# Retention and two feed-forward layers: the next pair's scores ahead of the outer products, and the work of the weights around them in another order

## Chip, cores and metric

One Trainium2 chip, one NeuronCore. The metric is device time in microseconds of the whole program; the runs shown of the kernel before have a median of 1027.86 us (1026.41, 1027.86 and 1028.14). The profile is one further execution.

## What is computed

```
def _attn_ref(q, k, v):                      # 4 batches, 8 heads, 768 positions, 64 wide
    for t in range(S):
        state = gamma * state + outer(k[:, :, t], v[:, :, t])
        y[:, :, t] = scale * q[:, :, t] @ state
def _moe_ref(x, w_in, w_out):                # 3072 tokens, 512 -> 2048 -> 512
    h = x @ w_in
    return np.maximum(0.01 * h, h) @ w_out
def _moe2_ref(x, w_in, w_out):               # the same shapes
    h = x @ w_in
    return (h * (1.0 / (1.0 + np.exp(-1.702 * h)))) @ w_out
reference = _moe2_ref(_moe_ref(tokens of _attn_ref, ...), ...)
```

The weights arrive as 64-bit floats, so each 512 KB piece of the first layer's weights has to be turned into single precision on the chip before it is used.

## The kernel before

**Retention.** The 768 positions of a batch are cut into 6 chunks of 128; 4 batches make 24 steps. Step s loads one block of 1 MB (`a_load`, L276): q and k with the head dimension on the partitions, then k and v by rows, 256 KB each. Five blocks lie in a ring (`in_ring`, the tile h in the rows). The parts of a step are:

- `a_scores` (L282): 16 matmuls into PSUM (L290) and the product with the decay mask on VectorE (L293) into one of two buffers
- `a_decay` (L296): 8 scalings of k on ScalarE (L301), not in a batch's last chunk
- `a_sum` (L313): 16 matmuls (L319) that add the chunk's k-v products to the state in PSUM; `a_state` (L330): the state scaled on VectorE (L333)
- `a_inner` (L322): 16 matmuls (L327) of the masked scores with v; `a_outer` (L336): 16 matmuls (L341) of q with the state, not in a batch's first chunk
- `a_store` (L346): the product with the decay of q on VectorE (L356, six instructions a pair, or L369, two a pair). Steps 0 to 3 are the first layer's input `x0`, which ScalarE (L365) and GpSimd (L157) also split into a high and a low part.

The main loop (L411) takes two steps, s and t = s + 1, a pair p = s / 2. In it, beside retention, 16 pieces of the first layer's weights (n = 0 to 15) are made ready: `load_raw` (L171) loads one into a ring of three; `work_scalar` (L210) makes two ScalarE passes (L178, L179) over it into a ring of three (`a_ring`); `work_vector` (L219) three VectorE passes (L182, L184, L186); `work_last` (L227) the rounding (L195, on GpSimd for the first two pieces, on VectorE after), four GpSimd subtractions for every second piece (L157) into `made`, and `finish` of the piece before (L197: a ScalarE cast L160 and a VectorE subtraction L157, high and low part of a matmul's weight). `factors_out` (L205) writes `made`, 512 KB, to DRAM from GpSimd's queue. `ffn_in` (L245) then multiplies a finished piece with `x0`: 12 matmuls (L253) into bank 7 or 0, a ScalarE pass (L257) and a DMA of 256 KB from ScalarE's queue.

Every engine executes its instructions in the order of the program text; nothing is reordered. In a pair that order is: scores of s and t; one piece's `work_scalar`, `work_vector`, `work_last`; the next piece's `work_scalar`; up to two `ffn_in`; sum and inner of s, its state; the next piece's `work_vector`; inner and sum of t; outer of s; state of t; outer of t; decays of the next pair; store of s; the next piece's `work_last`; store of t; loads of two later steps.

```
        loads = {0: (4, 5), 2: (6, 7), 4: (8, 9), 6: (10, 11, 12)}.get(s, (s + 5, s + 6))
```

The sixteen `ffn_in` stand in pairs 3 to 11 (`now_in`, L203). Behind the loop, the same weights are multiplied with `x1` (L1010), and two layers follow that take most of the time and that the diff does not touch.

Of the kernel before, what the change touches and what calls it, by code (L numbers as in the profile page):

```python
# [25 lines left out]
NC = S // P  # L26
KF = DFF // P
TB = 512
CPB = TB // P
N_STEPS = B * NC  # L30
# [27 lines left out]
QT = 2 * P  # L58
# [32 lines left out]
def retention_two_ffn(ctx: ExitStack, tc: tile.TileContext, qkv, consts, small, w1i, w1o, w2i, w2o, scratch, out):  # L91
    nc = tc.nc
# [63 lines left out]
    def subtract(o, x, y, e=nc.vector):  # L156
        e.tensor_tensor(out=o, in0=x, in1=y, op=ALU.subtract)  # L157

    def split(hi, lo, src, eng=nc.vector):
        nc.scalar.copy(out=hi, in_=src)  # L160
        subtract(lo, src, hi.bitcast(F32), eng)
# [9 lines left out]
    def load_raw(m):  # L171
        raw[m] = t = next(raw_ring).bitcast(U32)
        nc.sync.dma_start(out=t, in_=w1i[m].bitcast(U32).rearrange("p (f two) -> p f two", two=2))
# [20 lines left out]
    def round_up(f, low, e=nc.vector):  # L194
        e.tensor_tensor(out=f.bitcast(I32), in0=f.bitcast(I32), in1=low.bitcast(I32), op=ALU.add)  # L195
# [3 lines left out]
        wt[m] = t = home["h1"].view(8 * (m % NQ) + 4 * (m // NQ), 2, 512)  # L199
        split(t[:, 0], t[:, 1], a)  # L200

    P0 = 2
    now_in = {p: [m for m in (2 * p - 7, 2 * p - 6) if 0 <= m < KF] for p in range(N_STEPS // 2)}  # L203

    def factors_out(q):  # L205
        nc.gpsimd.dma_start(out=wdt[q], in_=made)

    made = e4.view(0, 4, QT)

    def work_scalar(n):  # L210
        if n + 2 < KF:
            load_raw(ORDER1[n + 2])
        if n < KF:
            t = raw.pop(ORDER1[n])
            a = next(a_ring).bitcast(U32)
            words_scalar(a, t[:, :, 0], t[:, :, 1])
            conv[ORDER1[n]] = a, t[:, :, 0], t[:, :, 1]

    def work_vector(n):  # L219
        if n < KF:  # L220
            a, _, high = conv[ORDER1[n]]
            for step in words_vector:
                step(a, high)
        if n and n % 2 == 0 and n <= KF:
            factors_out(n // 2 - 1)

    def work_last(n):  # L227
        if n < KF:
            a, low, _ = conv[ORDER1[n]]
            round_up(a, low, nc.gpsimd if n < 2 else nc.vector)  # L230
            f = a.bitcast(F32)
            if n % 2:
                b11, b21 = work_last.f[:, :QT], work_last.f[:, QT:]
                b12, b22 = f[:, :QT], f[:, QT:]
                for o, x, y in ((made[:, 3], b12, b11), (made[:, 2], b12, b22), (made[:, 1], b22, made[:, 3]),
                                (made[:, 0], b21, made[:, 1])):
                    subtract(o, x, y, nc.gpsimd)
            work_last.f = f
        if 0 < n <= KF:
            finish(ORDER1[n - 1])  # L240

# [3 lines left out]
    def ffn_in(m, x, cols, ring, queue=nc.scalar):  # L245
        n = cols.stop - cols.start
        h = banks[:, h_banks[i_h[0] % len(h_banks)], :n]
        i_h[0] += 1
        w = wt[m].rearrange("p s (k f) -> p s k f", k=NP)
        i = 0  # L250
        for k in range(NP):
            for a, c in ((0, 1), (0, 0), (1, 0)):
                nc.tensor.matmul(out=h, lhsT=w[:, a, k], rhs=x[c][:, k], start=(i == 0), stop=(i == 3 * NP - 1),  # L253
                                 skip_group_check=True)
                i += 1
        t = next(ring)[:, :n]
        nc.scalar.activation(out=t, in_=h, func=AF.Lrelu)  # L257
        queue.dma_start(out=gd1[m][:, cols], in_=t)

    def retention():  # L260
# [12 lines left out]
        ins, sc_t, ks_t = {}, {}, {}  # L273
        kv = banks[:, 2, : NP * D].rearrange("p (n d) -> p n d", n=NP)

        def a_load(s):  # L276
            ins[s] = next(in_ring)
            parts = ((0, 2), (3, 4)) if steps[s][1] == NC - 1 else ((0, 2), (2, 4)) if s < 3 else ((0, 4),)
            for i, j in parts:
                nc.sync.dma_start(out=ins[s][:, i:j], in_=qkv[s, :, i:j])  # L280

        def a_scores(s):  # L282
            t = ins[s]
            qT = t[:, 0].rearrange("p (n i) -> p n i", n=NP)
            kT = t[:, 1].rearrange("p (n i) -> p n i", n=NP)
            ps = (banks[:, 5:7] if s % 2 else banks[:, 0:2]).rearrange("p e (n i) -> p e n i", n=NP)
            for n in range(NP):
                for e in range(2):
                    r = slice(D * e, D * e + D)
                    nc.tensor.matmul(out=ps[:, e, n], lhsT=kT[r, n], rhs=qT[r, n], start=True, stop=True,  # L290
                                     skip_group_check=True)
            sm = next(sm_ring)
            nc.vector.tensor_tensor(out=sm, in0=ps, in1=mask, op=ALU.mult)  # L293
            sc_t[s] = sm
# [51 lines left out]
        def a_store(s, o):  # L346
            b, c = steps[s]
            if c % 3 == 0:
                a_store.x = next(x_ring)
            blk = min(s // CPB, 2) if s < NC else 2  # L350
            cols = slice(s * P, s * P + P)
            x = x1_raw[:, :, s % CPB * P : s % CPB * P + P] if blk == 1 else a_store.x[:, :, c % 3 * P : c % 3 * P + P]

            def put(r, u, t):
                n = 2 * P
                nc.vector.tensor_tensor(out=x[r].rearrange("p (m u) i -> p u m i", u=2)[:, u],  # L356
                                        in0=o[t, u, :n].rearrange("p (m i) -> p m i", i=P),
                                        in1=qdec[t].rearrange("p (m u) i -> p u m i", u=2)[:, u], op=ALU.mult)

            if blk < 2 or b == B - 1:  # L360
                put(slice(0, P), 0, slice(0, P))
                for r, t in halves:
                    put(r, 1, t)
            if blk == 0:
                nc.scalar.copy(out=x0[0][:, :, cols], in_=x)  # L365
                subtract(x0[1][:, :, cols], x, x0[0][:, :, cols].bitcast(F32), nc.gpsimd)
            if blk < 2 or b == B - 1:
                return
            nc.vector.tensor_tensor(out=x.rearrange("p (m u) i -> p u m i", u=2),  # L369
                                    in0=o[:, :, : 2 * P].rearrange("p u (m i) -> p u m i", i=P),  # L370
                                    in1=qdec.rearrange("p (m u) i -> p u m i", u=2), op=ALU.mult)
            if c % 3 == 2:
                a_store.due = xd0[b][c // 3], a_store.x
# [22 lines left out]
            for _ in range(n):  # L396
                nc.tensor.matmul(out=warm, lhsT=idle[:, :P], rhs=idle, start=True, stop=True, skip_group_check=True)

        def a_end(s, o):
            a_store(s, o)  # L400
            if a_store.due:
                nc.sync.dma_start(out=a_store.due[0].rearrange("n p c -> p n c"), in_=a_store.due[1])
                a_store.due = None

        keep_warm(8)
        a_scores(0)
        a_decay(0)
        a_decay(1)
        last = len(steps)
        units = iter(range(KF + 1))  # L410
        for s in range(0, last, 2):  # L411
            t, p = s + 1, s // 2
            mine = [n for n in itertools.islice(units, 2)] if p >= P0 else []
            if s:
                a_scores(s)
                a_scores(t)
            if mine:
                work_scalar(mine[0])
                work_vector(mine[0])
                work_last(mine[0])  # L420
            if len(mine) > 1:
                work_scalar(mine[1])
            i_h[0] = 0
            for m in now_in[p]:
                ffn_in(ORDER1[m], x0, slice(0, TB), g_ring)
            if not s:
                keep_warm(6)
            a_sum(s)
            a_inner(s)
            a_state(s)  # L430
            if not s:
                a_scores(t)
                keep_warm(6)
            if len(mine) > 1:
                work_vector(mine[1])
            a_inner(t)
            a_sum(t)
            o = a_outer(s)
            a_state(t)
            o2 = a_outer(t)  # L440
            for k in (s + 2, s + 3):
                if k < last:
                    a_decay(k)
            a_end(s, o)
            if len(mine) > 1:
                work_last(mine[1])
            a_end(t, o2)
            loads = {0: (4, 5), 2: (6, 7), 4: (8, 9), 6: (10, 11, 12)}.get(s, (s + 5, s + 6))
            for n, k in enumerate(loads):
                if k < last:  # L450
                    a_load(k)
                if n == 0 and s in (0, 2):
                    load_raw(ORDER1[s // 2])
            if p in (3, 4):
                k = slice(2 * p - 6, 2 * p - 4)
                split(x1[0][:, k], x1[1][:, k], x1_raw[:, k])
            for k in (s, t):
                for step in beside_steps.get(k - last, ()):
                    step()
# [864 lines left out]
```

## Time and profile before

| what | value |
|---|---|
| median of the runs shown | 1027.86 us |
| the profiled execution's own time | 1025.9 us |
| its span | 1024.2 us |
| TensorE busy | 1008.8 us, 99% |
| VectorE busy | 812.9 us, 79% |
| ScalarE busy | 607.9 us, 59% |
| GpSimd busy | 175.6 us, 17% |
| mean DMA rate | 232 GB/s |
| end of the retention loop on TensorE | 133.78 us |

The span runs from the first to the last instruction. Busy time counts an instruction from its start to its modelled end. The time that matters for this change lies in the first 134 us, which are read from rows in order of time on each engine: start, length, line, tiles, and in square brackets how long the engine stood idle ahead of the row and what ended that.

### The profile page before, as it was taken

How to read it: one execution, taken by the hardware profiler on the slowest of the kernel's cores; microseconds unless marked ns; L12 is line 12 of the kernel's file. 1: busy time of each engine (PE TensorE's matmuls, PEld its weight loads, DVE VectorE, ACT ScalarE, POOL GpSimd, SP SyncE). 2: the span in 40 equal slices, each digit the busy share in tenths (PEclk: the TensorE clock that was granted, in tenths of full speed). 3: DMA queues.
4: the chain of work that ended last, by engine and by line, in shares of the span. 5: the costliest groups of instructions: out<-in, count | busy, mean ns of one | idle time of the engine just before them, and what ended most of it. 6: DMA issues, size and time to landing. Idle time of an engine off the chain costs nothing.

```text
span 1024.2 us, 17017 instructions
## 1 busy us (share of the span) xinstructions
PE 1008.8 (99%) x5857; PEld 866.3 (85%) x5857; DVE 812.9 (79%) x1396; ACT 607.9 (59%) x1197; POOL 175.6 (17%) x304
## 2 busy tenths in 40 slices
PE   8899999999999999999999999999999999999998
PEld 6687799999999888888888888888888888888886
DVE  4988788987875998998989775554676997988986
ACT  5766556675666665555547765545666555455452
POOL 2432223333333000000000222222232000000000
PEclk9999999999999999999999999999999999999999
DMA  9899959979787846537454984664797646536524
GB/s 352 338 367 390 346 185 314 373 246 327 247 303 284 297 124 223 184 121 262 162 164 171 335 298 161 211 246 147 251 342 271 220 125 146 164 111 143 164 75 83
DMA packets 163814, 237.36 MB, mean 232 GB/s; under 512 B 58768, under 2 KB 103568, under 8 KB 161552
## 3 DMA queue, kind: packets, MB, share of 16 engines
q1 hardware_dynamic: 137408, 161.65, 49.2%
q0 software_dynamic: 19104, 69.62, 17.6%
q10 hardware_dynamic: 7216, 5.02, 1.5%
q8 instruction: 46, 0.75, 0.3%
q14 instruction: 40, 0.33, 0.1%
HBM read 143.95 MB, written 92.27 MB: 231 GB/s over the span
## 4 chain that ended last, share of the span: by engine, by line
PE 89%; DVE 4%; DMA 2%; ACT 2%; POOL 1%; issue 1%; ACTq 0%; DVEq 0%; POOLq 0%
PE psum L837 45%; PE psum L646 38%; PE psum L253 3%; ACT h L301 1%; DMA c<-w1i 1%; POOL e L157 1%; DVE b L293 1%; PE psum L327 1%; DMA wdt<-e 1%; DVE a L356 1%; PE psum L319 0%; PE psum L290 0%; DMA h<-qkv 0%; DVE h L157 0%; PE psum L341 0%
## 5 line engine op out<-in xcount | busy, mean ns | idle before, releaser
L837 PE MATMUL psum<-c,h 128*128 128x512 f32 x1008 | 228.9, 389 | 0.0
L837 PEld LDWEIGHTS psum<-c,h 128*128 128x128 f32 x1008 | 189.1, 188 | 39.2
L837 PE MATMUL psum<-b,h 128*128 128x512 f32 x768 | 179.3, 389 | 0.0
L837 PEld LDWEIGHTS psum<-b,h 128*128 128x128 f32 x768 | 144.2, 188 | 29.9
L659 POOL DMA_DIRECT2D gd<-e x107 | 58.1, 544 | 403.9 <-ACT e L668 383.9
L646 PE MATMUL psum<-d,h 128*128 128x384 f32 (+1 forms) x576 | 126.7, 362 | 0.0
L646 PEld LDWEIGHTS psum<-d,h 128*128 128x128 f32 x576 | 104.7, 188 | 11.2
L646 PE MATMUL psum<-c,h 128*128 128x512 f32 x384 | 102.3, 389 | 0.0
L157 DVE TENSOR_TENSOR h<-h 128x256 fp32r<-128x256 f32 (+3 forms) x158 | 72.4, 491 | 30.0 <-ACT h L561 27.5
L790 ACT CAST c<-a 128x512 fp32r<-128x512 f32 x96 | 59.3, 621 | 50.5 <-PE psum L837 27.3
L646 PEld LDWEIGHTS psum<-c,h 128*128 128x128 f32 x384 | 72.1, 188 | 15.0
L646 PE MATMUL psum<-b,h 128*128 128x384 f32 x432 | 83.0, 334 | 0.1
L668 ACT ACTIVATE e<-psum 128x512 f32<-128x512 f32 x72 | 43.1, 599 | 66.9 <-PE psum L646 40.3
L646 PE MATMUL psum<-e,h 128*128 128x384 f32 (+1 forms) x336 | 76.2, 342 | 0.0
L646 PEld LDWEIGHTS psum<-b,h 128*128 128x128 f32 x432 | 75.4, 188 | 0.6 <-DVE b L157 0.4
L157 DVE TENSOR_TENSOR c<-a,c 128x512 fp32r<-128x512 f32 x96 | 65.1, 687 | 11.2 <-ACT c L790 10.3
L646 PE MATMUL psum<-a,h 128*128 128x512 f32 x288 | 69.2, 389 | 0.0
L646 PEld LDWEIGHTS psum<-a,h 128*128 128x128 f32 x288 | 54.1, 188 | 11.2
L646 PEld LDWEIGHTS psum<-e,h 128*128 128x128 f32 x336 | 59.6, 188 | 1.8
L837 PE MATMUL psum<-e,h 128*128 128x512 f32 x210 | 53.6, 390 | 0.0
L837 PEld LDWEIGHTS psum<-e,h 128*128 128x128 f32 x210 | 39.3, 188 | 8.0
L790 ACT CAST c<-d 128x512 fp32r<-128x512 f32 x48 | 29.8, 622 | 26.7 <-PE psum L837 19.9
(203 smaller groups left out, 1688.8 us busy)
## 6 DMA issues: line engine op xcount, KB each, us to landing
gd<-e POOLq DMA_DIRECT2D x96, 256.0 KB, 3.8
a<-gd SPq DMA_DIRECT2D x72, 256.0 KB, 4.3
d<-gd SPq DMA_DIRECT2D x72, 256.0 KB, 4.4
h<-qkv SPq DMA_DIRECT2D x17, 1024.0 KB, 9.4
c<-w1i SPq DMA_DIRECT2D x16, 512.0 KB, 9.8
c<-w1o SPq DMA_DIRECT2D x32, 256.0 KB, 5.8
b<-w2o SPq DMA_DIRECT2D x32, 256.0 KB, 5.0
wd2o<-b POOLq DMA_DIRECT2D x16, 448.0 KB, 4.5
```

Of the source, the lines that this page charges most:

```text
L157: e.tensor_tensor(out=o, in0=x, in1=y, op=ALU.subtract)
L253: nc.tensor.matmul(out=h, lhsT=w[:, a, k], rhs=x[c][:, k], start=(i == 0), stop=(i == 3 * NP - 1), skip_group_check=True)
L293: nc.vector.tensor_tensor(out=sm, in0=ps, in1=mask, op=ALU.mult)
L301: nc.scalar.activation(out=ks_t[s][:, h], in_=ks_t[s][:, h], func=AF.Copy, scale=kdec[:, c, h : h + 1])
L327: nc.tensor.matmul(out=out(n, e), lhsT=v[:, n, r], rhs=sm[:, e, n], start=(n < 2 and s % 2 == 0), stop=(c == 0), skip_group_check=True)
L356: nc.vector.tensor_tensor(out=x[r].rearrange("p (m u) i -> p u m i", u=2)[:, u], in0=o[t, u, :n].rearrange("p (m i) -> p m i", i=P), in1=q ...
L646: nc.tensor.matmul(out=t, lhsT=w(k, a), rhs=x[b][:, k], start=(start and m == 0), stop=(m == 5), skip_group_check=True)
L659: put = lambda: nc.gpsimd.dma_start(out=self.dst[f * NQ + q][:, cols], in_=t)
L668: nc.scalar.activation(out=dst, in_=src, func=AF.Gelu_apprx_sigmoid)
L790: nc.scalar.copy(out=t[:, 0], in_=self.block_of(*item))
L837: nc.tensor.matmul(out=t[:, j], lhsT=w[:, j, a], rhs=x[:, b], start=(new and q == 0 and m == 0), stop=(q == NQ - 1 and m == 2), skip_group ...
```

## The change

In each pair the scores of the next pair (and their decays) move from the start of that pair to a place between the sums and the outer products of this one (`ahead`); in the first pair they stay behind the stores. The rounding moves into `work_vector`, ahead of the decays in program order, and the second piece's whole `work_vector` stands in the middle of the pair, the first piece's behind the stores. A load of 1 MB is cut in two: k and v as soon as the sums and inner products are through with the old block, q behind the outer products. The four subtractions' results are stored in two halves of 256 KB, and the halves go round three places. The `ffn_in` stand one pair earlier, and the pair's order is closed by them.

```diff
-    now_in = {p: [m for m in (2 * p - 7, 2 * p - 6) if 0 <= m < KF] for p in range(N_STEPS // 2)}
-    made = e4.view(0, 4, QT)
+    now_in = {p: [m for m in (2 * p - 5, 2 * p - 4) if 0 <= m < KF] for p in range(N_STEPS // 2)}
+    made = ring([(e4, 0), (e4, 2), (ins_a, 40)], 2, QT)
...
     def work_vector(n):
         if n < KF:
-            a, _, high = conv[ORDER1[n]]
+            a, low, high = conv[ORDER1[n]]
             for step in words_vector:
                 step(a, high)
+            round_up(a, low, nc.gpsimd if n < 2 else nc.vector)
+        if n + 3 < KF:
+            load_raw(ORDER1[n + 3])
...
+                u, v = next(made), next(made)
+                subtract(u[:, 1], b12, b11, nc.gpsimd)
+                subtract(u[:, 0], b12, b22, nc.gpsimd)
+                nc.gpsimd.dma_start(out=wdt[n // 2][:, 2:], in_=u)
+                subtract(v[:, 1], b22, u[:, 1], nc.gpsimd)
+                subtract(v[:, 0], b21, v[:, 1], nc.gpsimd)
+                nc.gpsimd.dma_start(out=wdt[n // 2][:, :2], in_=v)
...
+        load_raw(ORDER1[0])
+        a_load(4)
+        load_raw(ORDER1[1])
+        def ahead(s):
+            for k in (s + 2, s + 3):
+                if k < last:
+                    a_decay(k)
+            for k in (s + 2, s + 3):
+                if k < last:
+                    a_scores(k)
         for s in range(0, last, 2):
             t, p = s + 1, s // 2
+            n = 2 * p - 2
...
             a_state(s)
...
+            if n > 0:
+                work_vector(n - 1)
             a_inner(t)
             a_sum(t)
+            for k in (s + 5, s + 6):
+                if k < last:
+                    a_load(k, 0)
+            if s:
+                ahead(s)
+            outs = [a_outer(s)]
             a_state(t)
+            outs.append(a_outer(t))
+            for k, o in zip((s, t), outs):
+                a_store(k, o)
+            if not s:
+                ahead(s)
+                load_raw(ORDER1[2])
+            for k in (s + 5, s + 6):
+                if k < last:
+                    a_load(k, 1)
...
+            if n >= 0:
+                work_scalar(n)
+                work_vector(n)
+            i_h[0] = 0
+            for m in now_in[p]:
+                ffn_in(ORDER1[m], x0, slice(0, TB), g_ring)
+                if m == 2 * p - 5:
+                    work_scalar(n + 1)
+            if p and not now_in[p] or now_in[p] == [0]:
+                work_scalar(n + 1)
```

How the change moves instructions is shown at three places.

SyncE's DMA queue in the first pair, before, behind the loads of step 2 (h is the ring of blocks, c the raw weights; 128x2048 is a whole block of 1 MB, the first row steps 3 and 4):

```order
L280 DMA h_83<-qkv 128x2048 x2
L173 DMA c_222<-w1i 128x1024
L280 DMA h_83<-qkv 128x1024
L280 DMA h_83<-qkv 128x512
L280 DMA h_83<-qkv 128x2048
L173 DMA c_222<-w1i 128x1024
L280 DMA h_83<-qkv 128x2048
```

Step 5 is the third and fourth row there (k by rows is not loaded for a batch's last chunk), step 6 the fifth. The same queue at the same place in the change:

```order
L280 DMA h_82<-qkv 128x2048
L173 DMA c_131<-w1i 128x1024
L280 DMA h_82<-qkv 128x2048
L173 DMA c_131<-w1i 128x1024
L280 DMA h_82<-qkv 128x512 x2
L280 DMA h_82<-qkv 128x1536
L173 DMA c_131<-w1i 128x1024
L280 DMA h_82<-qkv 128x512 x2
```

All three raw pieces now stand in the first pair, and the q of step 5 (the first of the last row's two) is behind the third of them and behind most of step 6.

VectorE in the second pair (steps 2 and 3), as one piece of the difference from the masked scores of steps 2 and 3 to the stores of both (a, b and f are areas of the on-chip memory, psum the banks):

```order
 L293 TENSOR_TENSOR b<-psum,b 128x1024 x2
-L333 TENSOR_TENSOR b<-psum,f 128x256 x2
+L333 TENSOR_TENSOR b<-psum,f 128x256
+L293 TENSOR_TENSOR b<-psum,b 128x1024 x2
+L333 TENSOR_TENSOR b<-psum,f 128x256
 L356 TENSOR_TENSOR a<-psum,f 128x2x128
 L356 TENSOR_TENSOR a<-psum,f 64x2x128 x2
 L356 TENSOR_TENSOR a<-psum,f 128x2x128
 L356 TENSOR_TENSOR a<-psum,f 64x2x128 x2
```

The masked scores of steps 4 and 5 now stand ahead of the stores of steps 2 and 3.

VectorE in the change from the masked scores of steps 6 and 7 to the state of step 6 (d is the area of `x1`, g the third place of `a_ring`):

```order
L293 TENSOR_TENSOR b<-psum,b 128x1024 x2
L356 TENSOR_TENSOR d_78<-psum,f 128x2x128
L356 TENSOR_TENSOR d_78<-psum,f 64x2x128 x2
L356 TENSOR_TENSOR d_78<-psum,f 128x2x128
L356 TENSOR_TENSOR d_78<-psum,f 64x2x128 x2
L182 TENSOR_SCALAR g<-g 128x512
L184 TENSOR_SCALAR c_131<-g 128x512
L186 SCALAR_TENSOR_TENSOR g<-g,c_131 128x512
L195 ISA g<-c_131,g 128x1024
L157 TENSOR_TENSOR h_376<-b,h_376 128x512
L333 TENSOR_TENSOR b<-psum,f 128x256
```

Before, the four rows of stores (of steps 4 and 5) stood ahead of these masked scores; the rest of the stretch is the same.

## Rows read from the trace of the kernel before

**Rows 1.** The page's 40 slices of the span, busy tenths of the DMA engines.

```profile
DMA  9899959979787846537454984664797646536524
```

**Rows 2.** Stretches: busy us (instructions) of PE, PEld, DVE, ACT, POOL; clock; DMA share; GB/s.

```profile
16.90:40.69 23.79, 18.06 (x302) 14.81 (x300) 21.23 (x36) 17.27 (x52) 11.59 (x11) 1.00 0.89 349
40.69:133.78 93.09, 89.82 (x1156) 74.98 (x1156) 76.63 (x122) 56.21 (x153) 26.57 (x35) 1.00 0.95 348
133.78:160.00 26.22, 26.22 (x214) 26.22 (x211) 24.66 (x48) 17.26 (x39) 10.30 (x19) 1.00 0.71 229
```

**Rows 3.** TensorE in order of time: two rows that it waited for.

```profile
40.69 0.69 PE L319 MATMUL psum<-h 128*64 128x64 f32 x16 [2.10 <-DVE b L333]
...
83.14 0.47 PE L253 MATMUL psum<-d,h 128*128 128x512 f32 x1 [1.89 <-DVE b L293]
```

**Rows 4.** SyncE's queue in order of time, first pairs.

```profile
9.77 0.33 SPq L173 DMA_DIRECT2D c<-w1i  x1
10.39 4.50 SPq L280 DMA_DIRECT2D h<-qkv  x3
14.94 0.42 SPq L173 DMA_DIRECT2D c<-w1i  x1
```

**Rows 5.** DMA issues, 9.7 to 10 us, then 14.9 to 15.5: size, us to landing.

```profile
c<-w1i SPq DMA_DIRECT2D x1, 512.0 KB, 10.6
...
c<-w1i SPq DMA_DIRECT2D x1, 512.0 KB, 11.2
```

**Rows 6.** TensorE in order of time, the parts of steps 8 and 9.

```profile
50.23 1.92 PE L327 MATMUL psum<-b,h 128*64 128x128 f32 x32
51.98 0.63 PE L319 MATMUL psum<-h 128*64 128x64 f32 x16
52.55 1.10 PE L341 MATMUL psum<-h,b 64*64 64x128 f32 x32
53.58 2.06 PE L290 MATMUL psum<-h 64*128 64x128 f32 x32
55.56 0.50 PE L253 MATMUL psum<-d,h 128*128 128x512 f32 x1
```

**Rows 7.** VectorE in order of time, second to fourth pair.

```profile
22.20 2.62 DVE L356 TENSOR_TENSOR a<-psum,f 128x256 f32<-128x256 f32 x6
24.85 2.35 DVE L293 TENSOR_TENSOR b<-psum,b 128x1024 f32<-128x1024 f32 x2
27.12 0.42 DVE L182 TENSOR_SCALAR b<-b 128x512 f32<-128x512 f32 x1
...
28.65 0.42 DVE L333 TENSOR_TENSOR b<-psum,f 128x256 f32<-128x256 f32 x1
28.98 1.47 DVE L182 TENSOR_SCALAR b<-b 128x512 f32<-128x512 f32 x1
...
39.62 0.69 DVE L157 TENSOR_TENSOR h<-b,h 128x512 fp32r<-128x512 f32 x1
40.22 0.42 DVE L333 TENSOR_TENSOR b<-psum,f 128x256 f32<-128x256 f32 x1
```

**Rows 8.** ScalarE in order of time, second pair.

```profile
19.14 2.02 ACT L301 ACTIVATE h<-h,f 128x64 f32<-128x64 f32 x8 [0.29 <-DMA h<-qkv]
...
24.85 0.62 ACT L365 CAST c<-a 128x512 fp32r<-128x512 f32 x1 [0.71 <-DVE a L356]
25.38 0.66 ACT L178 ACTIVATE b<-c 128x512 f32<-128x512 f32 x1
```

**Rows 9.** GpSimd in order of time, second and third pair.

```profile
24.22 2.62 POOL L157 TENSOR_TENSOR d<-a,c 128x512 fp32r<-128x512 f32 x2 [3.29 <-ACT c L365]
28.87 1.29 POOL L195 TENSOR_TENSOR b<-b,c 128x512 int32<-128x512 int32 x1 [2.04 <-DVE b L186]
```

**Rows 10.** The chain that ended last, one piece: start, length, line.

```profile
83.14 2.96 PE psum L253 x12
```

**Rows 11.** The page's DMA issues: size, median us to landing.

```profile
h<-qkv SPq DMA_DIRECT2D x17, 1024.0 KB, 9.4
```

More of the change, by code (lines that the diff above doesn't have):

```diff
@@ L200, in finish @@
         split(t[:, 0], t[:, 1], a)
-    P0 = 2
-    now_in = {p: [m for m in (2 * p - 7, 2 * p - 6) if 0 <= m < KF] for p in range(N_STEPS // 2)}
-    def factors_out(q):
-        nc.gpsimd.dma_start(out=wdt[q], in_=made)
-    made = e4.view(0, 4, QT)
+    now_in = {p: [m for m in (2 * p - 5, 2 * p - 4) if 0 <= m < KF] for p in range(N_STEPS // 2)}
+    made = ring([(e4, 0), (e4, 2), (ins_a, 40)], 2, QT)
     def work_scalar(n):
-        if n + 2 < KF:
-            load_raw(ORDER1[n + 2])
         if n < KF:
@@ L220, in work_vector @@
         if n < KF:
-            a, _, high = conv[ORDER1[n]]
+            a, low, high = conv[ORDER1[n]]
             for step in words_vector:
                 step(a, high)
-        if n and n % 2 == 0 and n <= KF:
-            factors_out(n // 2 - 1)
-    def work_last(n):
+            round_up(a, low, nc.gpsimd if n < 2 else nc.vector)
+        if n + 3 < KF:
+            load_raw(ORDER1[n + 3])
         if n < KF:
-            a, low, _ = conv[ORDER1[n]]
-            round_up(a, low, nc.gpsimd if n < 2 else nc.vector)
             f = a.bitcast(F32)
             if n % 2:
-                b11, b21 = work_last.f[:, :QT], work_last.f[:, QT:]
+                b11, b21 = work_vector.f[:, :QT], work_vector.f[:, QT:]
                 b12, b22 = f[:, :QT], f[:, QT:]
[L235 to L238, printed above, removed]
+                u, v = next(made), next(made)
[5 more added lines that the diff above has]
+                nc.gpsimd.dma_start(out=wdt[n // 2][:, :2], in_=v)
+            work_vector.f = f
         if 0 < n <= KF:
@@ L274, in retention, with a_load @@
         kv = banks[:, 2, : NP * D].rearrange("p (n d) -> p n d", n=NP)
-        def a_load(s):
-            ins[s] = next(in_ring)
-            parts = ((0, 2), (3, 4)) if steps[s][1] == NC - 1 else ((0, 2), (2, 4)) if s < 3 else ((0, 4),)
+        def a_load(s, part=None):
+            if part != 1:
+                ins[s] = next(in_ring)
+            if part is None:
+                parts = ((0, 2), (2, 4)) if s < 3 else ((0, 4),)
+            elif part:
+                parts = ((0, 1),)
+            else:
+                parts = ((1, 2), (3, 4)) if steps[s][1] == NC - 1 else ((1, 4),)
             for i, j in parts:
@@ L397, in keep_warm @@
                 nc.tensor.matmul(out=warm, lhsT=idle[:, :P], rhs=idle, start=True, stop=True, skip_group_check=True)
[L399 to L403, printed above, removed]
         keep_warm(8)
@@ L409, in retention @@
         last = len(steps)
-        units = iter(range(KF + 1))
+        load_raw(ORDER1[0])
[8 more added lines that the diff above has]
+                    a_scores(k)
         for s in range(0, last, 2):
             t, p = s + 1, s // 2
[L413 to L425, printed above, removed]
+            n = 2 * p - 2
             if not s:
@@ L433, in retention @@
                 keep_warm(6)
-            if len(mine) > 1:
-                work_vector(mine[1])
+            if n > 0:
+                work_vector(n - 1)
             a_inner(t)
             a_sum(t)
-            o = a_outer(s)
-            a_state(t)
-            o2 = a_outer(t)
-            for k in (s + 2, s + 3):
-                if k < last:
[L443 to L453, printed above, removed]
+            for k in (s + 5, s + 6):
[4 more added lines that the diff above has]
+            outs = [a_outer(s)]
+            a_state(t)
+            outs.append(a_outer(t))
[5 more added lines that the diff above has]
+            for k in (s + 5, s + 6):
+                if k < last:
+                    a_load(k, 1)
+            if a_store.due:
+                nc.sync.dma_start(out=a_store.due[0].rearrange("n p c -> p n c"), in_=a_store.due[1])
+                a_store.due = None
             if p in (3, 4):
```

## The prediction

> **What bounds the kernel now.** I read the busy time by stretch first, then each engine in order of time, then the DMA issues. The change touches only the retention loop, so the question is when TensorE leaves it, at 133.78 us, and what happens behind. Behind it TensorE is busy for all of 26.22 us [rows 2], so whatever the loop gains or loses passes on to the end one for one, as long as its successors are not late. The granted clock is 1.00 in all three stretches, the upper level of 2.4 GHz, so no clock is to be won.
>
> In the loop TensorE stands idle for 93.09 - 89.82 = 3.27 us between 40.69 and 133.78 us, and for 23.79 - 18.06 = 5.73 us between 16.90 and 40.69 [rows 2]. That is all there is to win: 9.0 us, 0.9%. The later idle time is what the new place of the scores bears on. Its largest piece, 1.89 us at 83.14, is a matmul into bank 0 that waits until VectorE has read the scores there [rows 3]; with the scores taken half a pair earlier, that wait has no place. The earlier idle time ends with 2.10 us at 40.69, where the second sum of the fourth pair waits for a state on VectorE [rows 3].
>
> VectorE is the tight engine there: 21.23 of 23.79 us [rows 2]. It works in program order, so an instruction that waits holds up everything behind it. The DMA engines are full almost from the start: nine tenths or more in four of the first five slices [rows 1]. So two things decide the first 40 us: which load comes when, and what stands behind it on VectorE.
>
> **Part 1: the later pairs, -3.3 us.** TensorE's parts last, from one start to the next: two inner 1.75, a sum 0.57, two outer 1.03, two scores 1.98 us [rows 6]; twelve matmuls of an `ffn_in` 2.96 [rows 10]. A full pair with two of them takes about 1.75 + 1.1 + 1.03 + 1.98 + 5.9 = 11.8 us. In the new order the masked scores are needed only behind outer products and `ffn_in`, 1.03 + 5.9 us after the last score matmul; VectorE needs 2.35 us for them [rows 7]. VectorE's own work in such a pair: two states 0.84, two pieces of three passes at 27.12 to 28.65 = 1.53 each, with rounding and subtraction 0.69 each (the row of the subtraction; I take the rounding as equal), masks 2.35, stores up to 2.62: 11.6 at most [rows 7], so it just keeps pace. I take the whole 3.27 us as won; the bounds are 0 and 3.27.
>
> **Part 2: the first four pairs, +6.5 us.** This is the larger term. I follow it step by step.
>
> *The q of step 5.* Before, the first raw piece lands at 9.77 + 10.6 = 20.4 us and the second at 14.94 + 11.2 = 26.1 [rows 4, 5]. Between them lie step 5 (0.79 MB), step 6 (1.05) and that piece (0.52), 2.36 MB in 5.8 us, so 0.41 MB a microsecond, one transfer behind another. Step 5 is on the chip at about 20.4 + 0.79 / 0.41 = 22.3 us. In the change steps 0 to 4 and the first piece, the same set, are there at about 20.4; then come the second piece (0.52), k and v of step 5 (0.52), most of step 6 (0.79), the third piece (0.52) and only then the q of step 5 (0.26): 2.62 MB, so 26.8 us. The scores of step 5 cannot start before.
>
> The first pair's two casts now stand ahead of the decays of steps 2 and 3 on ScalarE. With 2.02 us a decay [rows 8] from about 17.8 us, steps 2 to 4 are through at 23.8, so this is hidden by the wait until 26.8 and costs nothing itself. If step 5 came at 22.3 it would show, by about 1 us.
>
> *From there to the state of step 6.* Scores of step 5 end at 27.9, their mask at 29.15, the state of step 3 at 29.55. Only now do the six stores of steps 2 and 3 run, 2.62 us, to 32.1; before they ended at 24.8 [rows 7]. ScalarE's casts follow (0.62), the last from 32.15, then its pass over piece 0 (0.66, started 0.53 behind) ends at 33.4 [rows 8]. GpSimd splits the two casts until 34.05 (2.62 for two) [rows 9].
>
> VectorE's first pass over piece 0 comes at 33.4, beside GpSimd. Before, such a pass took 0.42 us alone and 1.47 us where GpSimd worked at the same time, from 28.87 to 30.16 [rows 7, 9]: it lasted until GpSimd was through. The Trainium skill, SBUF — State Buffer, on the doors and their contention, calls the port pair of the two engines an exclusive lock held for a whole instruction; by that a pass waits in full, as in the row, and by a mere sharing of bandwidth the sum would be some 1.5 us smaller. I take the row. So: passes over piece 0 from 34.05 to 35.55, state of step 4 at 35.95; rounding of piece 0 on GpSimd 1.29 to 36.9 [rows 9]; passes over piece 1 held till then, done at 38.5; the low part of piece 0 at 39.1; masks of steps 6 and 7 at 41.4; stores of steps 4 and 5, which now stand here, at 44.0; three passes, rounding and subtraction of the next pieces at 46.7; state of step 6 at 47.15. Before it ended at 40.64 [rows 7]. TensorE's second sum of the fourth pair starts at 47.2 instead of 40.69: **+6.5 us**. Without any hold of VectorE by GpSimd it is about +5.0. That is the range of this step if the q lands where I put it; with the q at 24.5 it would be some 2.3 less.
>
> **Part 3: the smaller edits.** Halves in three places let GpSimd go on without waiting for a store. That wait was off TensorE's way except through ScalarE, whose delays are in the 3.27 us already. 8 more stores and 19 more loads are issued; SyncE's issue of 0.33 to 0.42 us [rows 4] lies beside the transfers. On the queue, whole, half and quarter blocks between the two raw pieces flowed at 0.41 MB a microsecond without a gap between them [rows 4, 5], so I cost the smaller transfers at nothing. [...] The `ffn_in` one pair earlier change nothing in TensorE's work.
>
> **The sum.** +6.5 - 3.3 = +3.2 us on the profiled execution: 1025.9 + 3.2 = 1029.1. The median of the runs shown is 2.0 us above the profiled execution, so I forecast 1027.86 + 3.2 = **1031.1 us**, 0.3% slower. A measurement of this kernel tells about 0.2%, 2.1 us, from no change.
>
> **Rivals.**
>
> *Faster: the start does not lose.* If the q of step 5 is served before the bulk queued ahead of it and is on the chip by 23 us, VectorE's masks are not held, the second and third pair keep their times and only the gain of part 1 stays: 1027.86 - 3.3 = 1024.6 us; with the wait of 2.10 us at 40.69 gone as well, 1022.5. For it: all transfers run on the same 16 engines, and the change asks for loads early. Against: the two raw pieces of rows 4 and 5 landed in the order of issue, spaced by the bytes between. It decides at a start of step 5's scores before about 24.5 us. Chance 0.20.
>
> *No difference.* The start loses about half of what I count, because the hold by GpSimd or the queueing is milder: +3.3 - 3.3 gives 1027.9 us. Chance 0.25.
>
> *Slower still: loads come too late in every pair.* An odd step's block is now issued when its old block is released in the middle of a pair and is needed in the middle of the next, for the q part 10 to 11 us later; the median block takes 9.4 us to land [rows 11]. If the cut loads take 11.5 us, TensorE waits some 0.7 us in each of seven pairs on top of the forecast: 1031.1 + 5 = 1036 us. For it: the DMA engines are full until the sixth slice [rows 1]. Against: the change's DMA time is the same and starts the middle pairs ahead of TensorE. Chance 0.10.
>
> **How the numbers follow.** The forecast, 1029 to 1033 us, has 0.45. Slower by over 0.2% (over 1029.9): the forecast and the last rival, 0.55. Within 0.2%: 0.25. Faster (below 1025.8): 0.20. The range has to reach into both neighbours: from 1025.0, which leaves out most of the faster rival, to 1035.0. The likeliest case's own range is 1029 to 1033.
>
> **What would show it.** In the profile after: scores of step 5 starting near 27 us behind a DMA; the stores of steps 2 and 3 at about 29.5 to 32 us; a wait of about 3 us of TensorE for the state of step 6, ending near 47; from there to the loop's end next to no idle time, and the end at about 137 us. If scores of step 5 start before 24.5 us, part 2 is wrong from its first step. If TensorE waits for the scores' loads in the later pairs, part 1 is wrong. If the loop ends before 132 us, the forecast is wrong altogether; if it ends at 137 and the program gains, the passing on behind it is.

## The result, and the profile after

The changed kernel takes 1036.59 us in the median of its runs (1034.02 to 1040.81), the kernel before 1027.86 (1026.41 to 1029.22): a ratio of 1.0094 (1.0065 to 1.0124), so it is slower by 0.9%. The forecast was 1031.1 us. The profiled execution took 1039.5 us, its span is 1037.8 us against 1024.2. TensorE is busy for 1016.6 us of it (1008.8 before), the mean DMA rate is 229 GB/s (232). It lies 2.9 us above its median and the profiled one of before 2.0 below, so the profiles differ by 13.6 us where the medians differ by 8.7. The runs differ along with their granted clock: 1034.02 us at 0.998, 1036.59 at 0.994, 1040.81 at 0.992 in the mean of a run.

Where the 13.6 us lie is told by the stretches. The first three rows answer to [rows 2]: up to the second sum of the fourth pair, from there to the loop's end, and behind it.

```profile
16.90:48.83 31.93, 21.12 (x309) 17.20 (x305) 22.28 (x36) 18.83 (x58) 11.88 (x12) 0.95 0.70 259
48.83:147.78 98.95, 94.92 (x1157) 80.14 (x1157) 73.91 (x122) 57.28 (x159) 31.18 (x42) 0.93 0.89 329
147.78:174.00 26.22, 26.22 (x212) 26.22 (x212) 24.65 (x48) 17.33 (x39) 10.29 (x19) 1.00 0.69 232
50.00:60.00 10.00, 8.72 (x58) 7.12 (x59) 7.43 (x12) 4.38 (x14) 4.36 (x6) 0.54 1.03 396
```

The sum starts at 48.83 instead of 40.69 us, 8.1 later. The later pairs take 98.95 instead of 93.09 us, 5.9 more. Together that is the 14.0 us by which the loop ends later; behind it TensorE is busy throughout, as before. Of the 5.9 us, 0.8 is idle time (98.95 - 94.92 = 4.03 against 3.27), and 5.1 is busy time: the same matmuls take 94.92 instead of 89.82 us, because the granted clock is at 0.93 in the mean. In the last row it is 0.54, near the lower level of 1.2 GHz.

TensorE in order of time, its waits (they answer to [rows 3]):

```profile
27.43 1.16 PE L290 MATMUL psum<-h 64*128 64x128 f32 x16 [4.00 <-DMA h<-qkv]
28.52 1.99 PE L341 MATMUL psum<-h,b 64*64 64x128 f32 x32
...
48.83 0.98 PE L319 MATMUL psum<-h 128*64 128x64 f32 x16 [2.07 <-DVE b L333]
49.74 2.08 PE L290 MATMUL psum<-h 64*128 64x128 f32 x16
53.10 2.08 PE L290 MATMUL psum<-h 64*128 64x128 f32 x16 [1.28 <-DMA h<-qkv]
...
92.10 1.16 PE L290 MATMUL psum<-h 64*128 64x128 f32 x16 [2.24 <-DMA h<-qkv]
...
116.62 1.16 PE L290 MATMUL psum<-h 64*128 64x128 f32 x16 [0.51 <-DMA h<-qkv]
```

The wait of 1.89 us at 83.14 for a score bank [rows 3] has no successor, as forecast. In its place the scores of steps 9, 15 and 19, all odd, wait for their blocks. The chain of waits shows the loads that ended last:

```profile
42.73 10.23 DMA h<-qkv
...
80.50 11.46 DMA h<-qkv
...
106.57 9.91 DMA h<-qkv
```

The one at 80.50 is the q of step 15. It landed at 91.96; TensorE was through with the scores of step 14 at 88.70 + 1.16 = 89.86, so a little under 9.4 us would have been in time. On SyncE's queue two raw pieces and k and v of both steps stand ahead of it:

```profile
74.18 4.53 SPq L173 DMA_DIRECT2D c<-w1i  x2
78.84 4.13 SPq L280 DMA_DIRECT2D h<-qkv  x4
...
85.03 4.73 SPq L173 DMA_DIRECT2D c<-w1i  x2
90.70 4.72 SPq L280 DMA_DIRECT2D h<-qkv  x5
```

It is the last load but one of the group at 78.84. The lower rows are those of the next pair: its block loads leave at 90.70, though the second sum had freed their place at about 88.7. The second raw piece, for whose place SyncE waits until VectorE's rounding, is issued ahead of them, at 89.43; for 0.9 us more SyncE waits for an earlier block to land.

VectorE in order of time, from the scores of step 5 to the state of step 6 (answers to [rows 7]):

```profile
28.64 1.22 DVE L293 TENSOR_TENSOR b<-psum,b 128x1024 f32<-128x1024 f32 x1 [3.94 <-PE psum L290]
29.78 0.41 DVE L333 TENSOR_TENSOR b<-psum,f 128x256 f32<-128x256 f32 x1
30.54 2.64 DVE L356 TENSOR_TENSOR a<-psum,f 128x256 f32<-128x256 f32 x6 [0.35 <-PE psum L341]
34.45 1.03 DVE L182 TENSOR_SCALAR b<-b 128x512 f32<-128x512 f32 x1 [1.27 <-ACT b L178]
...
36.92 1.45 DVE L182 TENSOR_SCALAR b<-b 128x512 f32<-128x512 f32 x1
...
42.35 2.61 DVE L356 TENSOR_TENSOR d<-psum,f 128x256 f32<-128x256 f32 x6
44.99 0.73 DVE L182 TENSOR_SCALAR g<-g 128x512 f32<-128x512 f32 x1
...
48.27 0.42 DVE L333 TENSOR_TENSOR b<-psum,f 128x256 f32<-128x256 f32 x1
```

### The profile page after: what moved, and what is told of

Same layout as the page of the kernel before. It is cut to its first block, busy times and chain, and to the rows that moved or that the text cites. A ratio compares the mean times of both kernels' runs of the same rounds, so it can differ in the third digit from the quotient of the medians.

```text
span 1037.8 us, 17086 instructions
## 1 busy us (share of the span) xinstructions
PE 1016.6 (98%) x5856; PEld 873.3 (84%) x5857; DVE 811.4 (78%) x1396; ACT 608.3 (59%) x1197; POOL 181.1 (17%) x312
## 4 chain that ended last, share of the span: by engine, by line
PE 89%; DMA 6%; DVE 3%; ACT 1%; issue 0%; ACTq 0%; SPq 0%
PE psum L843 41%; PE psum L652 38%; PE psum L247 6%; DMA h<-qkv 6%; PE psum L290 1%; PE psum L327 1%; PE psum L341 1%; PE psum L319 1%; DVE b L157 0%; DMA y<-c 0%; DVE d L157 0%; DVE c L1204 0%; DVE c L851 0%; DVE e L157 0%; DVE b L182 0%
## 5 line engine op out<-in xcount | busy, mean ns | idle before, releaser
L674 ACT ACTIVATE e<-psum 128x512 f32<-128x512 f32 x72 | 43.1, 598 | 65.6 <-PE psum L652 41.5
```

What stands on the lines that cost most here:

```text
L674: nc.scalar.activation(out=dst, in_=src, func=AF.Gelu_apprx_sigmoid)
```

## Experiments

Three things had to be told apart: the late start, the waits for loads later on, and the half clock. Ratios below are to the kernel before on the same chip.

| run | median us | ratio (95%) | sum of pair 4 at | later pairs, us |
|---|---|---|---|---|
| the kernel before | 1027.86 | | 40.69 | 93.1 |
| the changed kernel | 1036.59 | 1.0094 (1.0065 to 1.0124) | 48.83 | 99.0 |
| start's loads reordered | 1034.06 | 1.0059 (1.0042 to 1.0077) | 44.23 | 98.4 |
| odd step first, raw late | 1029.81 | 1.0015 (1.0006 to 1.0025) | 49.19 | 88.8 |
| both | 1026.43 | 0.9986 (0.9977 to 0.9995) | 46.03 | 90.0 |
| loads whole again | 1027.73 | 0.9997 (0.9988 to 1.0007) | 45.65 | 89.4 |
| idle matmuls in the waits | 1039.80 | 1.0111 (1.0092 to 1.0130) | 48.52 | 100.8 |
| raw late alone | 1030.49 | 1.0024 (1.0014 to 1.0034) | 49.54 | 90.0 |
| odd step first alone | 1030.35 | 1.0025 (1.0016 to 1.0034) | 49.15 | 89.2 |
| both, stores first in pair 2 | 1025.38 | 0.9966 (0.9957 to 0.9976) | 44.68 | 88.5 |
| the same, state of step 6 first | 1025.35 | 0.9970 (0.9958 to 0.9982) | 42.48 | 91.1 |
| whole loads, raw late, stores first | 1025.05 | 0.9971 (0.9959 to 0.9983) | 43.07 | 88.9 |
| before with halves | 1029.18 | 1.0013 (1.0001 to 1.0024) | 40.84 | 95.6 |

The two last columns are read from the profile of each run: the start of that row on TensorE, and from there to the loop's end.

### The loads of the first pair

```diff
         a_load(4)
-        load_raw(ORDER1[1])
...
                     a_load(k, 0)
+                if not s and k == 5:
+                    a_load(k, 1)
...
                 ahead(s)
+                load_raw(ORDER1[1])
+                a_load(6, 1)
                 load_raw(ORDER1[2])
             for k in (s + 5, s + 6):
-                if k < last:
+                if s and k < last:
                     a_load(k, 1)
```

> Only the order of the loads in the first pair differs from the changed kernel: step 5 is loaded whole as soon as its place is free, then k and v of step 6, and the second and third raw piece follow behind. Theory A (the late q of step 5 holds up VectorE's queue and so the first four pairs): scores of step 5 start near 23 us instead of 27.4, the second sum of the fourth pair near 44 to 45 instead of 48.8, and the program takes 4 us less than the changed kernel, about 1032 us, and some more less if TensorE's clock then stays up in the later pairs. Rival (VectorE is late because the stores, the rounding and the masks stand in another order, whatever the loads do): the sum stays at 48 us or later and the time at 1036 us.

The scores of step 5 run with those of step 4 from 22.15 us, without a wait, and the sum starts at 44.23 instead of 48.83: 4.6 us earlier, as theory A has it. The median falls by 2.5 us only, with intervals that overlap (1.0042 to 1.0077 against 1.0065 to 1.0124), since the later pairs keep their waits for loads:

```profile
48.95 2.08 PE L290 MATMUL psum<-h 64*128 64x128 f32 x16 [2.81 <-DMA h<-qkv]
...
86.77 2.08 PE L290 MATMUL psum<-h 64*128 64x128 f32 x16 [2.25 <-DMA h<-qkv]
```

So the order of the first pair's loads, which made that q late, was the cause of somewhat over half the loss at the start (4.6 of 8.1 us), and the later loss is a thing of its own.

### The loads of the later pairs

First both bulks are taken from ahead of the odd step's q: the even step's k and v, and the raw piece that `work_vector` loads in the middle of the pair. Both now come behind the stores.

```diff
-        if n + 3 < KF:
+        if n + 3 < KF and n % 2 == 0:
             load_raw(ORDER1[n + 3])
...
-                if k < last:
+                if k < last and (not s or k == s + 5):
                     a_load(k, 0)
...
                 if k < last:
+                    if s and k == s + 6:
+                        a_load(k, 0)
                     a_load(k, 1)
+            if n > 0 and n + 2 < KF:
+                load_raw(ORDER1[n + 2])
```

> Only later pairs differ from the changed kernel: k, v and q of the odd step are issued ahead of the even step's block, and the raw piece of the middle of the pair behind both. Theory B (the odd step's q is late because it stands behind the raw piece and 768 KB of a step that is not wanted yet): no wait of TensorE's scores for a load behind 55 us, the start as in the changed kernel (sum at about 48.8 us), the granted clock at 1.00 from 60 us on, the loop's end 3 to 6 us earlier, program 1031 to 1034 us. Rival C (the loads are late because DMA is full, in whatever order): the waits remain, on other steps, and the time is 1036 us.

Then each alone: only the lines on `load_raw`, or only those on `a_load`.

> The changed kernel with one load moved: the raw piece of the middle of a pair is issued behind the pair's block loads. If that piece, which holds up SyncE's queue until VectorE's rounding releases its place, is what makes the odd step late, the waits for loads in the later pairs go and the time is that of the run with the odd step first, about 1030 us. If it is the 768 KB of the even step ahead of the odd step's q, the waits stay and the time is 1034 to 1037 us. I expect a part of each: waits of under 1.5 us and 1032 to 1034 us.

> The counterpart of the run with the raw piece late: the changed kernel with the odd step's k, v and q ahead of the even step's block, and the raw piece of the middle of the pair left in front of them. If that raw piece in SyncE's queue is needed for the waits, they stay, and the time is 1034 us or more. If either of the two bulks ahead of the odd q is enough to make it late, and taking either away is enough to cure it, the waits go here too and the time is 1029 to 1031 us. I expect the second: by the bytes 768 KB ahead are 1.9 us, the raw piece 1.3 us.

The later pairs with both moved, in the view by stretch:

```profile
49.19:138.00 88.81, 88.73 (x1157) 75.56 (x1157) 73.67 (x122) 57.04 (x159) 31.41 (x42) 1.00 0.95 358
```

The waits are gone, and the clock stays at 1.00. The start is as late as ever, so this is the later loss alone: 10 us between the two profiles, 6.8 between the medians, more than the 3 to 6 us expected. The bytes are the same, so rival C falls. Moving either bulk alone gives nearly all of it (90.0 us with the raw piece late, 89.2 with the odd step first, with one wait of 1.34 and one of 0.46 us left); of the raw piece alone I had expected less. Theory B holds in a milder form: neither is the culprit; both together put the odd q past the 9.4 us that it has.

> Both reorderings of loads together. Theories A and B: sum of the fourth pair at 44 to 45 us, no later wait for a load, no stretch at the lower clock behind 50 us; loop's end about 135 to 137 us, program 1026 to 1030 us. Rivals: 1034 to 1036 us.

Both reorderings: 1026.43 us, at the lower end of what was expected, and no wait for a load is left:

```profile
46.03:136.05 90.02, 90.02 (x1156) 76.93 (x1156) 73.91 (x122) 57.29 (x159) 30.95 (x42) 0.98 0.94 353
```

The later pairs take 1.2 us more than with the start left alone; at a clock of 0.98 they are busy time throughout. The sum came at 46.03 us, where 44 to 45 was expected and the first run had 44.23. This too is the clock: up to there both runs have the same work on TensorE and VectorE, but behind the first sum of the second pair the same inner matmuls ran at the lower level, and the scores behind them start at 23.96 instead of 22.15. TensorE in the run with the start's loads reordered, then twice in this one:

```profile
19.84 1.80 PE L327 MATMUL psum<-b,h 128*64 128x128 f32 x30
...
20.19 3.38 PE L327 MATMUL psum<-b,h 128*64 128x128 f32 x31
...
46.65 3.43 PE L290 MATMUL psum<-h 64*128 64x128 f32 x32
```

The last row, the scores of steps 8 and 9, takes 2.06 us at the upper level [rows 6].

In the next run, again against the changed kernel, a block is loaded whole, in the place where the q was.

```diff
-                parts = ((0, 2), (2, 4)) if s < 3 else ((0, 4),)
+                parts = ((0, 2), (3, 4)) if steps[s][1] == NC - 1 else ((0, 2), (2, 4)) if s < 3 else ((0, 4),)
...
-            for k in (s + 5, s + 6):
-                if k < last:
-                    a_load(k, 0)
...
-                    a_load(k, 1)
+                    a_load(k)
```

> The cut of the loads is undone: each block is loaded whole behind the stores, as in the kernel before; the rest is the changed kernel. If the cut itself (more and smaller transfers, and the q apart) is what costs, the program comes to 1028 to 1031 us. If the new place of the scores is what costs, because they need the block half a pair earlier, the waits for loads get longer than in the changed kernel (over 2 us in several pairs) and the time is 1036 us or more. I lean to the second, at 1036 to 1042 us.

Here I was wrong: whole loads, issued later, take 1027.73 us, 9 us less than the changed kernel, some 3 of them at the start (45.65 against 48.83). The odd step's megabyte then has nothing of the even step ahead of it, and that outweighs its later issue; the one wait left in the later pairs is 0.69 us at 81.80. The scores half a pair earlier are thus no cost where the loads come in time.

### The half clock

```diff
+        fill = {5: 15, 9: 5, 15: 9}
...
                 if k < last:
+                    keep_warm(fill.get(k, 0))
                     a_scores(k)
...
+            if t == 7:
+                keep_warm(8)
             a_sum(t)
```

> The changed kernel with idle matmuls (on a zero tile, into a bank that nobody reads then) in the four places where TensorE waits long: 15 ahead of the scores of step 5, 8 ahead of the second sum of the fourth pair, 5 and 9 ahead of the scores of steps 9 and 15. Theory C (the half clock is a cost of its own, some 5 us, and follows from TensorE's idle stretches): the granted clock is 1.00 in 50 to 60 us, the waits for loads and the state stay, the loop ends 3 to 6 us earlier and the program takes 1031 to 1033 us. Rival (the half clock only fills time in which TensorE would wait anyway): 1036 us, the waits longer by what the matmuls gain.

The matmuls kept the clock at 1.00 from 40 to 114 us, and the program did not gain. The later pairs, the stretch that ran at 0.54 in the changed kernel, and a stretch behind the filled places:

```profile
48.52:149.35 100.83, 95.44 (x1170) 79.40 (x1171) 73.95 (x122) 57.41 (x159) 30.83 (x42) 0.97 0.87 323
50.00:60.00 10.00, 8.15 (x65) 6.06 (x62) 7.69 (x12) 5.57 (x16) 4.37 (x6) 1.00 1.03 397
114.00:122.00 8.00, 6.62 (x55) 5.58 (x56) 4.01 (x7) 2.16 (x6) 3.00 (x5) 0.57 1.04 416
```

The clock is 1.00 from 50 to 60 us, and the scores of step 9 start at 53.33 instead of 53.10 all the same. What TensorE gained behind them it lost for the most part at the next loads: the scores of step 13 wait 0.54 us, where they had not, those of step 19 wait 2.85 instead of 0.51, and start at 115.38 instead of 116.62. There the clock falls after all. From these scores on no load is waited for, and the same 429 matmuls, without idle time in either run, take 2.8 us more than in the changed kernel. This run, then the changed kernel, from the scores of step 19 to the loop's end:

```profile
115.38:149.35 33.97, 33.97 (x429) 28.80 (x429) 20.15 (x35) 13.24 (x37) 6.32 (x9) 0.91 0.67 244
116.62:147.78 31.16, 31.16 (x429) 26.51 (x429) 21.43 (x37) 15.64 (x45) 8.42 (x12) 1.00 0.77 286
```

So the loop ends at 149.35 us, not earlier than 147.78, and theory C, which had it 3 to 6 us earlier, falls in that size. But the rival holds only as far as the loads set the pace: there the half clock fills time that would be waited through, and of what was gained 1.24 us are left at step 19. Where no load is waited for behind it, the half clock costs its time, as here and in the run with both reorderings. How much of the changed kernel's 5.1 us of busy time would come back if the clock alone stayed up to the loop's end was not tried.

### What is left at the start

```diff
-            if s:
+            if s > 2:
                 ahead(s)
...
                 a_store(k, o)
+            if s == 2:
+                ahead(s)
```

> The run with both reorderings of loads, and in the second pair the scores and decays of steps 4 and 5 behind the stores of steps 2 and 3, as in the kernel before. Theory D (what is left of the loss at the start is VectorE's order: the masks that wait for loads stand ahead of stores that could run): the six stores run from about 21.5 to 24.5 us while the scores wait, the second sum of the fourth pair starts at 42 to 43.5 us instead of 46.0, and the program takes 1022.5 to 1024.5 us. Rival (the chain of casts and GpSimd's hold set it): the sum stays near 46 us, 1026 us.

The time is 1025.38 us, faster than before by 0.34%, but the sum moved by 1.3 us only, where theory D had 2.5 to 4. Counted from the first sum of the second pair (19.84 us here, 18.26 in the run with both) it is 2.9 us, but half of that is the clock: the inner matmuls behind that sum took 1.80 us again, not 3.38. Against the first run, where they took 1.80 us too, 1.4 us are left for the order. The six stores ran at 25.13, not at 21.5: they wait for outer products whose sum waits for ScalarE's decays. The stretch from the sum to the loop's end has no idle time left:

```profile
44.68:133.13 88.45, 88.45 (x1157) 75.47 (x1157) 73.76 (x122) 57.04 (x159) 31.23 (x42) 1.00 0.95 360
```

Next, the state for which the sum still waited 2.05 us:

```diff
             a_state(s)
...
+            if s == 6:
+                work_vector(2)
...
-                work_vector(n)
+                if s != 4:
+                    work_vector(n)
```

> The run with the stores first, and at the turn from the third to the fourth pair the state of step 6 ahead of VectorE's passes over the third piece instead of behind them (its raw load moves with them). Theory D goes on: the second sum of the fourth pair waited 2.05 us at 44.7 for that state; without it the sum starts at about 42.6, the later pairs stay free of waits, and the program takes 2 us less, about 1023.5 us, 0.5% under the kernel before. Rival: the passes moved behind the state make the masks of steps 8 and 9 or the piece's matmuls late, the wait shows up there, and the time stays at 1025.4 us.

```profile
54.95 0.69 PE L319 MATMUL psum<-h 128*64 128x64 f32 x16 [1.18 <-DVE b L333]
56.36 2.06 PE L290 MATMUL psum<-h 64*128 64x128 f32 x32 [0.72 <-ACT d L251]
...
80.31 1.16 PE L290 MATMUL psum<-h 64*128 64x128 f32 x16 [0.22 <-DMA h<-qkv]
```

The sum starts at 42.48 without a wait, and waits come back behind it: two in the next pair, one more at 80.31, 2.1 us in all. The time is unchanged, as the rival had it. For the wait of 1.18 us a reason is at hand, that VectorE has the same work up to that point, so that taking one wait away moved it; this was not tried, and the other two are waits for ScalarE and for a load.

### The cut and the halves by themselves

The first of these joins edits shown above: whole loads, the lines on `load_raw` and the stores first. The second puts the change's lines on `u` and `v`, and the ring of three places, into the kernel before; the rest of that stays.

> Stores first in the second pair, blocks loaded whole behind the stores and the middle raw piece behind them: everything that helped, without the cut of the loads. If the cut is worth nothing by itself, the later pairs are free of waits and the time is that of the run with the stores first within 1 us, 1024.5 to 1026.5 us. If the earlier issue of k and v is needed, waits of the scores for loads of 0.5 to 1.5 us stay in some pairs and it is 1027 us or more. I expect the first.

With whole loads and all else that helped the ratio is 0.9971 (0.9959 to 0.9983), against 0.9966 (0.9957 to 0.9976) with cut ones. The two also differ in the order of the first pair's loads; the cut, with the order of loads that goes with it, is worth nothing that can be told, in either direction.

> The kernel before with one part of the change: the factors stored in two halves of 256 KB right behind their subtractions, in three places. Part 3 of the prediction: no change, 1027 to 1029 us, though GpSimd's waits for the stores go. Rival: with GpSimd free earlier, ScalarE's casts and passes come earlier and TensorE's idle 3.3 us shrink: 1025 to 1026.5 us.

GpSimd's waits for the stores of the factors, 41.5 us in all before, are gone from its waits. The ratio of 1.0013 (1.0001 to 1.0024) shows no gain, so the rival falls; a loss of 0.1 to 2.5 us fits it. In the profile TensorE waits for score banks 5.0 us in the later pairs, against 3.0 before; whether that comes of the halves, one profile does not tell.

## Why the prediction was wrong

**What bounds the kernel, and the passing on.** Right. The loop's end is 14.0 us later, the span 13.6.

**Part 1, -3.3 us: the step that failed.** It said "I take the whole 3.27 us as won". Measured are +5.9 us in the profiled execution; in the median run it is less, by an estimate +2.5, if the 6.8 us that the run with both bulks moved is faster are added to its 88.81 - 93.09 = -4.3. With the 8.1 us of the start that gives 1025.9 + 8.1 + 2.5 = 1036.5, the median: by this estimate the 2.0 us that the forecast put on top for the median did not come on top, and that hid a part of the miss. The old waits did vanish, all 3.27 us of them, those for score banks included. But part 1 counted the engines' work and left the loads out: three waits for them are 4.03 us. The other 5.1 us are busy time at the lower clock, which the prediction put at nothing: it read that "no clock is to be won" and did not ask what could be lost. For the odd step's q it gave only a rival, and there 10 to 11 us were set against a median of 9.4 [rows 11], taken from a kernel with other bytes ahead of each block. With the queue read in the new order, the raw piece (0.52 MB) and the even step's k and v (0.79 MB) stand, the one ahead of the odd step's block, the other between that and its q: at the 0.41 MB a microsecond that the prediction itself had used in part 2, 3.2 us. Done once for a later pair, that sum would have made more of the rival. Where the loads come in time, part 1 is right and even short: 93.09 - 88.45 = 4.6 us won, 3.27 of idle time and 1.4 of busy time, which I had not counted and whose cause stays open.

**Part 2, +6.5 us: right in mechanism, 1.6 short in size.** The scores of step 5 started at 27.43 (26.8 forecast), the state of step 4 at 36.59 and so ended at 37.0 (35.95), the masks of steps 6 and 7 ended at 42.4 (41.4), the state of step 6 ended at 48.7 (47.15). The error grows from 0.6 us at the load to 1.5: stores that wait 0.35 us for outer products (which ran at the lower clock, 32 in 1.99 us instead of 1.10), a first pass of 1.03 us, later ones of 0.73. That the sum follows the q one for one held: in the first run scores of step 5 some 4.2 us earlier gave 4.6. The other 3.5 us stay with the q early (44.23 against 40.69).

VectorE's first passes beside GpSimd lasted 1.03, 1.45 and 0.73 us, against 0.42 alone [rows 7]. GpSimd's rows at that time:

```profile
32.56 2.63 POOL L157 TENSOR_TENSOR d<-a,c 128x512 fp32r<-128x512 f32 x2 [13.40 <-ACT c L365]
36.81 1.28 POOL L195 TENSOR_TENSOR b<-b,c 128x512 int32<-128x512 int32 x1 [1.61 <-DVE b L186]
...
43.89 1.55 POOL L157 TENSOR_TENSOR e<-b,e 128x256 f32<-128x256 f32 x2
```

The passes end at 35.48, 38.37 and 45.72, GpSimd at 35.19, 38.09 and 45.44: each pass ends 0.3 us behind it. That is the full wait that the prediction took. The Trainium skill, SBUF — State Buffer (SBUF: two separate sides), calls the port pair that the two share an exclusive lock, and the rows agree. A mere sharing of bandwidth does not fit: shared evenly, by an estimate, the pass from 36.92 would end at about 37.8. No run took GpSimd's work away there, so what the hold costs the program was not tried.

**Part 3, nothing.** Right within some 0.2%. Halves alone gave 1.0013 (1.0001 to 1.0024), cut loads in their order 0.9966 against 0.9971 with whole ones. The Trainium skill, DMA: Bandwidth & Descriptors (Anatomy of one DMA — SWDGE (gpsimd) path), fits a fixed 2.0 us to each transfer that GpSimd issues, and puts most of it down to completion; the blocks leave from SyncE's queue, where these runs show no such cost of cutting a transfer.

**The rivals.** "Loads come too late in every pair", at 0.10 and 1036 us, came nearest in time and mechanism. Its argument against, that the DMA time is the same and starts ahead of TensorE, is where it was undervalued: the amount was the same, the order was not. Its price was built otherwise than what happened: three waits, not seven, with the half clock behind them.

## What to carry to other kernels

When work that needs a load is moved earlier, count for that load the bytes that stand ahead of it in the queue in the new order, and the waits of the issuing engine ahead of it; a median landing time of the old order does not tell when it lands. What is needed first goes first: the same transfers in another order made 1036.6 us into 1026.4. A low clock behind a wait is hidden as far as another wait follows, and is paid in full behind the last: look what TensorE waits for next before adding it or leaving it out.

## What was not expected of the hardware

The granted clock fell to the lower level during or behind idle stretches, but not behind all of them: TensorE stood idle for 2.07 us before 48.83 and 1.28 before 53.10, and ran at 0.54 from 50 to 60 us, so that 16 score matmuls took 2.08 us instead of 1.16. Before the change, a like wait of 2.10 us at 40.69 [rows 3] left the clock at 1.00 [rows 2]. With idle matmuls in those places it stayed at 1.00 there. In nine runs, the changed kernel among them, TensorE waits 2.05 to 2.07 us ahead of that same sum: in three of them (the changed kernel, start's loads reordered, both) the clock was at 0.52 to 0.63 in the next 4 to 6 us, in the six others it stayed at 1.00. What decides between the two these runs do not tell.
